# VectorE operands of a token search moved from SBUF to PSUM, in an attention and mixture-of-experts kernel

## The chip, the cores and the metric

The kernel runs on one core of a Trainium2 chip. Times are device microseconds of a whole execution of that core; the median of several runs counts. TensorE multiplies matrices, VectorE and ScalarE do elementwise work, GpSimd does elementwise work and issues the transfers with row lists, SyncE issues the other transfers.

## The reference

Three layers on 3072 tokens of 512 values, in float32: windowed attention, a dense layer, and a layer of 8 experts. The last one matters here:

```python
logits = x @ w_gate                      # 3072 x 8
order = np.argsort(-flat)                # all (token, expert) pairs, largest first
for idx in order:
    tok, e = (int(idx) // E, int(idx) % E)
    if assigned[tok] >= 0 or counts[e] >= cap:   # cap = 384
        continue
    assigned[tok] = e
    counts[e] += 1
...
for e in range(E):
    mask = assigned == e
    h = np.maximum(x[mask] @ w1[e], 0.0)         # 384 x 512 @ 512 x 1024
    out[mask] = h @ w2[e]                        # 384 x 1024 @ 1024 x 512
```

So each expert gets exactly 384 tokens, in the order of the logits.

## The kernel before, in words

Attention and the dense layer come first, in eight units of 384 tokens. The experts follow. The assignment does not sort: it finds which expert is full first, and with which tokens, and repeats this for the experts that are left. One such search (`search`, from L619) goes through eight levels of 16 thresholds on the 32-bit key of each token's best logit. `z[:, l]` holds digit l of 128 x 24 tokens. A level is:

- VectorE compares all tokens with 16 thresholds, in two halves, giving `mk` (L630 at the first level, L632 later);
- TensorE counts by expert, six products into `cnt` (L637);
- VectorE subtracts the digit found from `z[:, l]` (L640), carries it into the next digit (L642), and takes the own columns of `cnt` into `csum` (L644);
- TensorE sums these into `ct`, four products (L647);
- VectorE finds the digit `d` (`full` L652, `td` L654, L656).

After the eighth level `assign` (from L672) takes the expert `em`, its number `EI` (L683), its tokens `S`, and their running sums `sc` (L685). TensorE turns the sums of the partitions into offsets `off` (L690, L691). VectorE masks the expert's logits (L695), and `choose` (L997) makes every token's next best expert and its digits; ScalarE writes these into `z` (L1015). Then the slot list: positions `pos`, the tokens `mine`, the tokens done so far, two comparisons `ge` (L719), `row`, `cm`, `jc` (L730), and `oh` (L735), six operations of 128 x 512. From `oh` and `jc` TensorE makes the list `li` in 24 products (L739); VectorE reads it into `IDX` (L741, L743). With `IDX` GpSimd gathers the tokens' rows (L770) and, at the end, scatters the results (L834).

One search runs beside the products of the expert before. These are 96 products of 128 x 384 for the hidden layer (L811 to L813) and 72 of 128 x 512 for the output (L827 to L829). `beside` steps through the search: a step's TensorE instructions are tied behind a given product of the experts (`issue_after`), after as many nominal nanoseconds of products as `GAPS` names. Each engine runs its own instructions in a fixed order; a planner sets that order when the kernel is built. `limit` lets the search run up to two experts ahead.

An expert's weights come as 16 loads of 256 KB once `EI` is known and a buffer is free. ScalarE rounds each to the leading part (L762), GpSimd subtracts it for the trailing part (L763; for expert 0 half of them on VectorE). ScalarE and VectorE split the hidden layer likewise (`hh` L816, `hl` L817) and the gathered tokens (`mxh` L778, `mxl` L779). A finished expert's middle result is read out by VectorE (`res`, L833).

In PSUM, the bank `pS` ("search") holds `cnt`, `ct` and `off`; `li` has a bank of its own in the same pool; all other operands of the search are in SBUF.

Of the kernel before, what the change touches and what calls it, by code (L numbers as in the profile page):

```python
# [9 lines left out]
F32 = mybir.dt.float32  # L10
# [13 lines left out]
GRP = 4                       # columns of a group in the search  # L24
AHEAD = 3                     # quarters of w_in split before the first hidden unit
LEAD = 8                      # products by which the attention runs ahead of the dense layers
PACE0, PACE = 5000, 6000      # of the experts' weight loads, and from a load to its split
LAT0, LAT = 5000, 6000
TW, TR = (16000, 14000, 12000), 2000    # of the transposes of an expert's tokens
GAPS = (1600, 500, 1500, 6000)          # what the vector engine needs between the steps of the search  # L30
# [7 lines left out]
def attn_mlp_moe(ctx, tc, qT, kP, v, w_in, w_out, w_outT, w_gate, w1, w2, out):  # L38
# [31 lines left out]
    # lifetimes: `late` lasts to the end of the dense layers, `early` to the last hidden unit, `att` to the  # L70
    # last attention unit
# [13 lines left out]
    # masks over [previous block | sinks | own block], added to the negated scores  # L85
# [12 lines left out]
    # rows of head 0 / head 1 of a pair among the sink rows  # L98
# [18 lines left out]
    # a float64 weight is two words; its leading 24 bits become hi + lo  # L117
    WIN, WO = {}, {}

    def leading(pairs, n):  # L120
        """float32 of float64 word pairs: exponent rebased (the leading words, as float32, scaled by a power of
        two, so that what is too small becomes zero), mantissa cut to 23 bits"""
# [55 lines left out]
    # before the first hidden unit the banks of the dense layers serve the attention too  # L178
# [236 lines left out]
    def gate(u, c, ys):  # L415
        """logits of a unit, by quarters of its columns"""
# [11 lines left out]
    def logits(u):  # L428
        """from the products with the leading and the trailing part of the weights; then the choice"""
# [11 lines left out]
    # logits of the last unit straight from its hidden layer, by w_out @ w_gate, so that its assignment  # L441
    # runs beside its second product
# [51 lines left out]
    def pair_steps(u, p):  # L494
        """one head pair: a transpose follows the scores of the next block, so that the softmax has its time"""
# [21 lines left out]
    # the weights come between the loads of the first unit, and are split as they are needed  # L517
# [97 lines left out]
    ct, off = pS[:, 128:144], pS[:, 160:162]  # L615

    EI, IDX, NXT = {}, {}, {0: (BEST, CH, Z)}

    def search(n, best, ch, z, S):  # L619
        """the expert with the largest threshold, by digits; its tokens above the threshold and at it"""  # L620
        d = None
        for l in range(8):
            # tokens at or above every threshold
# [10 lines left out]
            # their number for every expert, by column of the group, then their sums  # L634
            for g in range(NJ // GRP):
                gs = slice(g * GRP, (g + 1) * GRP)
                nc.tensor.matmul(cnt, ch[:, gs].rearrange("p j e -> p (j e)"), mk[:, gs], start=(g == 0),  # L637
                                 stop=(g == NJ // GRP - 1))
            if l:
                dve.tensor_scalar(z[:, l], z[:, l], d, None, op0=OP.subtract)  # L640
            if l < 7:
                dve.scalar_tensor_tensor(z[:, l + 1], z[:, l], 16.0, z[:, l + 1], op0=OP.mult, op1=OP.add)  # L642
# [5 lines left out]
            # the digit of every expert's own search, then the largest  # L648
# [8 lines left out]
        # the expert  # L657
        es = wk.tile([P, E], F32, name="es")
        em = wk.tile([P, 1], F32, name="em")
        dve.scalar_tensor_tensor(es, td[:, :E], d, K["rank"], op0=OP.is_equal, op1=OP.mult)  # L660
        dve.tensor_reduce(em, es, AX.X, OP.max)
        # its tokens: above the threshold, at it
        above = wk.tile([P, NJ], F32, name="above")
        dve.tensor_scalar(above, z[:, 7], 16.0, d, op0=OP.mult, op1=OP.subtract)
# [7 lines left out]
    def assign(n, best, ch, z):  # L672
        """the next expert to fill up, and its tokens; what the next search needs"""
# [3 lines left out]
        else:  # L677
            # the rest is the last one's
# [5 lines left out]
        sc = wk.tile([P, 2, NJ], F32, name="sc")  # L684
        dve.tensor_tensor_scan(sc.rearrange("p h j -> p (h j)"), K["one1"], S.rearrange("p h j -> p (h j)"), 0.0,  # L685
# [6 lines left out]
        if n < E - 1:  # L692
            e1 = wk.tile([P, E], F32, name="e1")
            dve.tensor_scalar(e1, es, em, None, op0=OP.is_equal)
            dve.scalar_tensor_tensor(lm, e1[:, None, :].to_broadcast(V3), GONE, lm, op0=OP.mult, op1=OP.add)  # L695
            nxt = NXT[n + 1] = (wk.tile([P, NJ], F32, name="best"), wk.tile(V3, BF, name="ch"),
                   wk.tile([P, 8, NJ], F32, name="z", bufs=1))
            choose(nc, wk, K, lm, *nxt)
            z0 = nxt[2][:, 0]
            if n:  # L700
                dve.tensor_sub(z0, z0, done)
        # the first of those at the threshold, until it is full
        pos = wk.tile([P, 2, NJ], F32, name="pos")
        mine = wk.tile([P, NJ], F32, name="mine")
        dve.scalar_tensor_tensor(pos[:, 1], sc[:, 1], off[:, 1:2], S[:, 1], op0=OP.add, op1=OP.mult)
# [343 lines left out]
```

## Time and profile before

| | |
|---|---|
| median of 3 runs | 1345.03 us (1343.74 to 1352.11) |
| span of the profiled execution | 1342.2 us |
| TensorE busy in it | 1189.4 us (89%) |
| VectorE busy | 907.2 us (68%) |
| ScalarE busy | 606.9 us (45%) |
| GpSimd busy | 541.1 us (40%) |

The profile names lines as L632 and tiles as `mk<-z,d,steps`, which is output, then inputs. PE is TensorE, PEld its weight load, DVE VectorE, ACT ScalarE, POOL GpSimd. PEclk is the clock that was granted to TensorE, as a part of the full one. A time in brackets is what the engine waited before the instruction, and for whom. Windows are microseconds from the start of the span. "x7" is a run of seven instructions merged into one row.

### The profile page before, as it was taken

To read this page: it belongs to the slowest core of one execution; us is meant where nothing else is said; L and a number is where in the kernel's file an instruction comes from. 1 tells how busy PE (TensorE), PEld (TensorE's weight loads), DVE (VectorE), ACT (ScalarE), POOL (GpSimd) and SP (SyncE) were. 2 spreads that over 40 slices of the span, in tenths; PEclk is the share of its full clock that TensorE was granted. 3 is DMA by queue.
4 is the path that set the end of the run, shared out by engine and by line. 5 is a ranking of instruction groups with operands and counts; after the bars stand their busy time and mean duration, and the time that the engine had idled before them with its cause. 6 is when DMAs were issued, how large, how long until landed. Compare 5 with 4: busy or idle time off the path is not lost.

```text
span 1342.2 us, 19655 instructions
## 1 busy us (share of the span) xinstructions
PE 1189.4 (89%) x6484; PEld 979.2 (73%) x6484; DVE 907.2 (68%) x2320; ACT 606.9 (45%) x1436; POOL 541.1 (40%) x614
## 2 busy tenths in 40 slices
PE   4677899999999999999999999978759698787997
PEld 3466688888887878788888888646537476566996
DVE  7988976667667777756666545678777787776221
ACT  5755455566556556555566544033123241322411
POOL 6457633324334433523323310056262653725710
PEclk9988899999899999999999999979779798797999
DMA  6554433333424334333323220354142341434300
GB/s 223 169 178 150 165 126 93 97 90 124 114 95 128 118 102 124 112 86 93 98 89 95 76 71 1 103 172 148 49 126 73 101 142 63 142 104 132 110 24 24
DMA packets 87606, 145.29 MB, mean 108 GB/s; under 512 B 9680, under 2 KB 32208, under 8 KB 87504
## 3 DMA queue, kind: packets, MB, share of 16 engines
q1 hardware_dynamic: 83664, 131.45, 31.5%
q0 software_dynamic: 3840, 12.59, 2.8%
q8 instruction: 51, 0.84, 0.2%
q14 instruction: 51, 0.42, 0.1%
HBM read 127.22 MB, written 16.78 MB: 107 GB/s over the span
## 4 chain that ended last, share of the span: by engine, by line
PE 56%; DVE 23%; issue 8%; DMA 7%; POOL 3%; ACT 2%; SPq 1%; POOLq 0%; DVEq 0%; ACTq 0%
PE h L373 6%; PE h L371 5%; PE h L372 5%; PE y L400 5%; PE y L401 5%; PE y L399 5%; PE o L349 4%; DMA wtr<-in_w_outT_dram 3%; DVE mk L632 3%; PE h L811 2%; DMA wraw<-in_w_dram 2%; PE h L812 2%; PE t L317 2%; PE h L813 2%; DVE f L129 2%
## 5 line engine op out<-in xcount | busy, mean ns | idle before, releaser
L763 POOL TENSOR_TENSOR w<-wraw,w 128x512 fp32r<-128x512 f32 x120 | 171.0, 1458 | 185.7 <-ACT w L762 161.0
L371 PE MATMUL h<-xh,win 128*128 128x384 f32 x512 | 179.7, 352 | 0.7 <-ACT xh L361 0.7
L373 PE MATMUL h<-xh,win 128*128 128x384 f32 x512 | 178.7, 349 | 0.0
L372 PE MATMUL h<-xl,win 128*128 128x384 f32 x512 | 176.5, 345 | 0.0
L401 PE MATMUL y<-wo,gl 128*128 128x512 f32 x336 | 141.0, 421 | 1.6 <-DVE gl L385 1.6
L400 PE MATMUL y<-wl,gh 128*128 128x512 f32 x336 | 136.1, 405 | 0.0
L399 PE MATMUL y<-wo,gh 128*128 128x512 f32 x336 | 135.9, 405 | 0.0
L298 POOL TENSOR_SCALAR a<-a,stat 128x260 f32<-128x260 f32 (+2 forms) x168 | 87.2, 532 | 101.6 <-DVE stat L290 73.3
L286 ACT ACTIVATE a<-sm,stat 128x260 f32<-128x260 f32 (+2 forms) x192 | 94.6, 493 | 54.4 <-DVE stat L285 51.6
L816 ACT ACTIVATE hh<-h 128x384 fp32r<-128x384 f32 x64 | 31.4, 490 | 181.4 <-PE h L813 177.6
L262 POOL TENSOR_TENSOR vs<-vr,vs 128x192 fp32r<-128x192 f32 (+1 forms) x64 | 51.3, 809 | 145.7 <-ACT vs L261 145.3
L371 PEld LDWEIGHTS h<-xh,win 128*128 128x128 f32 x512 | 98.9, 193 | 6.4 <-ACT xh L361 1.6
L372 PEld LDWEIGHTS h<-xl,win 128*128 128x128 f32 x512 | 98.8, 193 | 5.4 <-issue 0.8
L378 DVE TENSOR_TENSOR g<-h,g 128x384 f32<-128x384 f32 x128 | 70.7, 552 | 44.5 <-ACT g L377 44.3
L373 PEld LDWEIGHTS h<-xh,win 128*128 128x128 f32 x512 | 98.5, 192 | 2.7 <-issue 1.8
L285 DVE CUSTOM_DVE_ANT_0 sm<-s,m 128x260 f32<-128x260 f32 (+2 forms) x192 | 76.5, 400 | 34.2 <-PE s L277 28.2
L811 PE MATMUL h<-mxh,w 128*128 128x384 f32 x256 | 97.9, 385 | 0.0
L762 ACT CAST w<-wraw 128x512 fp32r<-128x512 f32 x128 | 75.5, 619 | 46.5 <-DMA wraw<-in_w_dram 43.7
L248 POOL TENSOR_TENSOR kl<-k,kh 128x388 fp32r<-128x388 f32 (+1 forms) x64 | 84.5, 1327 | 26.7 <-ACT kh L247 26.3
L812 PE MATMUL h<-mxl,w 128*128 128x384 f32 x256 | 95.2, 373 | 0.0
L813 PE MATMUL h<-mxh,w 128*128 128x384 f32 x256 | 94.3, 369 | 0.0
L377 ACT ACTIVATE g<-h 128x384 f32<-128x384 f32 x128 | 62.1, 485 | 68.5 <-PE h L373 59.6
(257 smaller groups left out, 2996.7 us busy)
## 6 DMA issues: line engine op xcount, KB each, us to landing
wl<-wol_d SPq DMA_DIRECT2D x128, 256.0 KB, 2.9
wraw<-in_w_dram SPq DMA_DIRECT2D x128, 256.0 KB, 3.1
k<-in_k_dram SPq DMA_DIRECT2D x64, 131.0 KB, 2.9
winr<-in_w_in_dram SPq DMA_DIRECT2D x8, 1024.0 KB
wor<-in_w_out_dram SPq DMA_DIRECT2D x8, 1024.0 KB, 5.4
wtr<-in_w_outT_dram SPq DMA_DIRECT2D x8, 1024.0 KB
k<-in_k_dram SPq DMA_DIRECT2D x64, 97.0 KB, 2.5
q<-in_q_dram SPq DMA_DIRECT2D x32, 192.0 KB, 2.6
```

Source lines behind the costliest of these rows:

```text
L286: nc.scalar.activation(a[:, hh, :n], sm[:, :n], AF.Exp, bias=r[:, 0, hh:hh + 1], scale=-1.0, accum_out=r[:, 1, hh:hh + 1])
L298: nc.gpsimd.tensor_scalar(a[:, j, :n], a[:, j, :n], r[:, 3, j:j + 1], 1.0, op0=OP.mult, op1=OP.mult)
L371: nc.tensor.matmul(hp, w, xh[:, c], start=(c == 0), stop=False)
L372: nc.tensor.matmul(hp, w, xl[:, c], start=False, stop=False)
L373: nc.tensor.matmul(hp, win(f, 1, c), xh[:, c], start=False, stop=(c == NC - 1))
L399: yield 213, nc.tensor.matmul(y, gh[:, ts], hi, start=(f == 0), stop=False)
L400: yield 213, nc.tensor.matmul(y, gh[:, ts], lo, start=False, stop=False)
L401: yield 213, nc.tensor.matmul(y, gl[:, ts], hi, start=False, stop=(f == NF - 1))
L763: (dve if n == 0 and q % 2 else nc.gpsimd).tensor_sub(t[:, 1], r, raw(t)[:, 0])
L811: nc.tensor.matmul(hp, w1h[:, c], xh[:, c], start=(c == 0), stop=False)
L812: nc.tensor.matmul(hp, w1h[:, c], xl[:, c], start=False, stop=False)
L813: yield 480, nc.tensor.matmul(hp, w1l[:, c], xh[:, c], start=False, stop=(c == NC - 1))
```

## The change

Operands of the search move from SBUF to PSUM, so that operations with two tensors have one in each memory. A new bank `hold` (`pH`) takes `z`, `dg`, `val`, `best`, `row`, `above` and a copy of `rank`; the free columns of the bank `search` (`pS`) take the slot list `li`, copies of `shift` and of the scan's ones, `e1`, `sc`, `pos`, `mine`, `cm` and `em`. The bank that `li` had is given up. `z[:, l]` less the digit goes to a new SBUF tile `zd` instead of back into `z`. Two sums of SBUF pairs become reductions over a pair (`either`, `g2`). The tokens done are subtracted from the next `z` once, after they have been added up, so the subtraction of L701 goes. `row` becomes float32. Comments go as well. The core of the diff:

```diff
-    ct, off = pS[:, 128:144], pS[:, 160:162]
-
-    EI, IDX, NXT = {}, {}, {0: (BEST, CH, Z)}
+    ct, off, li = pS[:, 128:144], pS[:, 160:162], pS[:, 176:176 + 2 * NT].rearrange("p (h t) -> p h t", h=2)
...
+    pH = psS.tile([P, 512], F32, name="hold")
...
+    zH, dgH = held(pH, 0, 8, NJ), held(pH, 192, 8, NJ).bitcast(I32)
+    valH, bestH = held(pH, 384, NJ), (held(pH, 408, NJ), held(pH, 432, NJ))
+    rowH, aboveH, rankH = held(pH, 456, NJ), held(pH, 480, NJ), held(pH, 504, E)
+    oneS, e1S, shiftS = held(pS, 64, 2 * NJ), held(pS, 112, E), held(pS, 120, 8).bitcast(I32)
+    scS, pos1S, posS = held(pS, 192, 2, NJ), held(pS, 240, NJ), held(pS, 264, NJ)
+    mineS, cmS, emS = held(pS, 288, NJ), held(pS, 312, NJ, NT), held(pS, 384, 1)
+    for d, x in ((rankH, K["rank"]), (shiftS, K["shift"]), (oneS, K["one1"]), (zH, Z)):
+        nc.vector.tensor_copy(d, x)
+    KP = dict(K, rank=rankH, shift=shiftS)
+
+    EI, IDX, NXT = {}, {}, {0: (BEST, CH, zH)}
...
+            zd = wk.tile([P, NJ], F32, name="zd")
             if l:
-                dve.tensor_scalar(z[:, l], z[:, l], d, None, op0=OP.subtract)
+                dve.tensor_scalar(zd, z[:, l], d, None, op0=OP.subtract)
+            else:
+                dve.tensor_copy(zd, z[:, l])
             if l < 7:
-                dve.scalar_tensor_tensor(z[:, l + 1], z[:, l], 16.0, z[:, l + 1], op0=OP.mult, op1=OP.add)
+                dve.scalar_tensor_tensor(z[:, l + 1], zd, 16.0, z[:, l + 1], op0=OP.mult, op1=OP.add)
...
-        em = wk.tile([P, 1], F32, name="em")
-        dve.scalar_tensor_tensor(es, td[:, :E], d, K["rank"], op0=OP.is_equal, op1=OP.mult)
+        em = emS
+        dve.scalar_tensor_tensor(es, td[:, :E], d, rankH, op0=OP.is_equal, op1=OP.mult)
...
-        above = wk.tile([P, NJ], F32, name="above")
-        dve.tensor_scalar(above, z[:, 7], 16.0, d, op0=OP.mult, op1=OP.subtract)
+        above = aboveH
+        dve.tensor_scalar(above, zd, 16.0, d, op0=OP.mult, op1=OP.subtract)
...
-        sc = wk.tile([P, 2, NJ], F32, name="sc")
-        dve.tensor_tensor_scan(sc.rearrange("p h j -> p (h j)"), K["one1"], S.rearrange("p h j -> p (h j)"), 0.0,
+        sc = scS
+        dve.tensor_tensor_scan(sc.rearrange("p h j -> p (h j)"), oneS, S.rearrange("p h j -> p (h j)"), 0.0,
                                op0=OP.mult, op1=OP.add)
...
-            e1 = wk.tile([P, E], F32, name="e1")
+            e1 = e1S
...
-            nxt = NXT[n + 1] = (wk.tile([P, NJ], F32, name="best"), wk.tile(V3, BF, name="ch"),
-                   wk.tile([P, 8, NJ], F32, name="z", bufs=1))
-            choose(nc, wk, K, lm, *nxt)
-            z0 = nxt[2][:, 0]
-            if n:
-                dve.tensor_sub(z0, z0, done)
...
+            nxt = NXT[n + 1] = (bestH[n % 2], wk.tile(V3, BF, name="ch"), zH)
+            choose(nc, wk, KP, lm, *nxt, val=valH, dg=dgH)
+            z0 = zH[:, 0]
+
+        either = wk.tile([P, NJ], F32, name="either")
+        mine, pos = mineS, posS
+        dve.scalar_tensor_tensor(pos1S, sc[:, 1], off[:, 1:2], S[:, 1], op0=OP.add, op1=OP.mult)
+        dve.tensor_reduce(either, S.rearrange("p h j -> p j h"), AX.X, OP.add)
+        dve.scalar_tensor_tensor(mine, pos1S, CAP + 0.5, either, op0=OP.is_lt, op1=OP.mult)
         if n < E - 1:
-            dve.tensor_sub(z0, z0, mine)
             dve.tensor_add(done, done, mine)
+            dve.tensor_sub(z0, z0, done)
...
+        pos0 = wk.tile([P, NJ], F32, name="pos0")
+        dve.scalar_tensor_tensor(pos0, sc[:, 0], of0, S[:, 0], op0=OP.add, op1=OP.mult)
+        dve.tensor_add(pos, pos0, pos1S)
...
-        dve.tensor_add(g2, ge[:, 0], ge[:, 1])
-        row = wk.tile([P, NJ], BF, name="row")
-        dve.scalar_tensor_tensor(row, g2, -float(P), pos[:, 0], op0=OP.mult, op1=OP.add)
-        cm = wk.tile([P, NJ, NT], F32, name="cm", bufs=1)
+        dve.tensor_reduce(g2, ge.rearrange("p h j -> p j h"), AX.X, OP.add)
+        row = rowH
+        dve.scalar_tensor_tensor(row, g2, -float(P), pos, op0=OP.mult, op1=OP.add)
+        cm = cmS
         dve.tensor_sub(cm[:, :, 0], mine, ge[:, 0])
-        dve.tensor_sub(cm[:, :, 1], ge[:, 0], ge[:, 1])
+        dve.scalar_tensor_tensor(cm[:, :, 1], pos, 2 * P + 0.5, ge[:, 0], op0=OP.is_lt, op1=OP.mult)
...
-        li = psS.tile([P, 2, NT], F32, name="li")
...
-def choose(nc, pool, K, lm, best, ch, z):
+def choose(nc, pool, K, lm, best, ch, z, val=None, dg=None):
...
-    dg = pool.tile(D3, I32, name="dg", bufs=1)
-    nc.vector.tensor_tensor(dg, u[:, 1:2].to_broadcast(D3), K["shift"][:, :, None].to_broadcast(D3),
+    sh = pool.tile(D3, I32, name="dg", bufs=1)
+    if dg is None:
+        dg = sh
+    nc.vector.tensor_tensor(sh, u[:, 1:2].to_broadcast(D3), K["shift"][:, :, None].to_broadcast(D3),
                             op=OP.logical_shift_right)
     nc.vector.tensor_reduce(best, eq, AX.X, OP.max)
-    nc.vector.tensor_scalar(dg, dg, 15, None, op0=OP.bitwise_and)
+    nc.vector.tensor_scalar(dg, sh, 15, None, op0=OP.bitwise_and)
```

## Rows read from the trace of the kernel before

**Rows 1.** Busy us by engine (and instructions) per window, PEclk, DMA share, GB/s.

```profile
800.00:868.00 68.00, 68.00 (x403) 53.44 (x402) 37.92 (x139) 18.21 (x40) 0.12 (x1) 1.00 0.16 46
868.00:900.00 32.00, 22.69 (x139) 15.24 (x138) 27.64 (x89) 11.74 (x21) 19.23 (x11) 0.81 0.64 212
900.00:1250.00 350.00, 283.00 (x1613) 213.93 (x1612) 260.70 (x761) 97.29 (x187) 172.25 (x133) 0.85 0.33 105
1250.00:1342.00 92.00, 84.36 (x429) 75.68 (x427) 15.68 (x28) 21.29 (x42) 27.16 (x25) 0.98 0.16 52
```

**Rows 2.** Waits of TensorE, 900 to 1250 us: total us, times, longest.

```profile
PE search L637 <- DVE mk L632: 24.7, 6, 8.2
PE li L739 <- DVE oh L735: 19.2, 10, 6.5
PE search L647 <- DVE csum L644: 14.4, 5, 4.9
```

**Rows 3.** VectorE groups, 800 to 868 us: busy us, mean ns, idle before.

```profile
L632 DVE SCALAR_TENSOR_TENSOR mk<-Z,d,steps 128x192 bf16<-128x192 f32 x14 | 5.2, 416 | 0.3
...
L644 DVE TENSOR_TENSOR csum<-search,own 32x64 f16<-32x64 f32 x8 | 1.7, 212 | 0.8 <-PE search L637 0.8
...
L640 DVE TENSOR_SCALAR Z<-Z,d 128x24 f32<-128x24 f32 x7 | 1.7, 238 | 0.2
```

**Rows 4.** VectorE groups, 900 to 1250 us.

```profile
L632 DVE SCALAR_TENSOR_TENSOR mk<-z,d,steps 128x192 bf16<-128x192 f32 x74 | 60.6, 860 | 1.2
L735 DVE TENSOR_TENSOR oh<-slots,row 128x512 bf16<-128x512 bf16 x42 | 37.5, 956 | 0.0
L640 DVE TENSOR_SCALAR z<-z,d 128x24 f32<-128x24 f32 x38 | 25.2, 663 | 0.8
L817 DVE SCALAR_TENSOR_TENSOR hl<-h,hh 128x384 fp32r<-128x384 f32 x45 | 24.6, 547 | 15.5 <-ACT hh L816 15.2
...
L644 DVE TENSOR_TENSOR csum<-search,own 32x64 f16<-32x64 f32 x43 | 9.0, 210 | 20.7 <-PE search L637 20.2
...
L701 DVE TENSOR_TENSOR z<-z,done 128x24 f32<-128x24 f32 x6 | 6.5, 1086 | 2.0 <-ACT z L1015 2.0
...
L1005 DVE TENSOR_TENSOR eq<-LG,val 128x192 f32<-128x192 f32 x6 | 2.1, 350 | 0.0
```

**Rows 5.** Timelines of VectorE, GpSimd, TensorE around one stop: start, us.

```profile
937.67 9.15 DVE L632 SCALAR_TENSOR_TENSOR mk<-z,d,steps 128x192 bf16<-128x192 f32 x2
...
937.70 8.58 POOL L763 TENSOR_TENSOR w<-wraw,w 128x512 fp32r<-128x512 f32 x7
...
946.55 0.32 PE L637 MATMUL search<-mk,ch 128*32 128x64 bf16 x3 [8.23 <-DVE mk L632]
```

**Rows 6.** Windows after that stop, and a later one.

```profile
948.00:957.00 9.00, 9.00 (x38) 6.33 (x37) 3.98 (x18) 0.97 (x2) 0.00 (x0) 0.56 0.01 2
957.00:967.00 10.00, 10.00 (x68) 6.49 (x66) 6.95 (x29) 2.13 (x5) 1.09 (x2) 1.00 0.00 0
...
1034.00:1044.00 10.00, 9.20 (x70) 6.30 (x70) 7.90 (x19) 6.17 (x12) 10.00 (x5) 1.00 0.50 173
```

**Rows 7.** Timelines of TensorE and VectorE in one slot list.

```profile
1034.50 0.26 PE L739 MATMUL li<-jc,oh 128*128 128x6 bf16 x4 [0.54 <-DVE oh L735]
...
1035.36 0.26 PE L637 MATMUL search<-mk,ch 128*32 128x64 bf16 x3
...
1033.77 3.69 DVE L735 TENSOR_TENSOR oh<-slots,row 128x512 bf16<-128x512 bf16 x6
...
1039.39 0.16 DVE L743 SCALAR_TENSOR_TENSOR idx<-li,ls 128x3 int32<-128x3 f32 x1
```

**Rows 8.** VectorE's timeline: ends of two experts, a search's result.

```profile
1102.82 0.68 DVE L833 COPY res<-o 128x512 f32<-128x512 f32 x1
...
1135.34 0.13 DVE L683 TENSOR_SCALAR ei<-em 1x1 int32<-1x1 f32 x1
...
1165.42 0.68 DVE L833 COPY res<-o 128x512 f32<-128x512 f32 x1
```

More of the change, by code (lines that the diff above doesn't have):

```diff
@@ L614, in attn_mlp_moe, with held @@
     cnt = pS[:GRP * E, :GRP * 16].rearrange("p (j k) -> p j k", k=16)
-    ct, off = pS[:, 128:144], pS[:, 160:162]
-    EI, IDX, NXT = {}, {}, {0: (BEST, CH, Z)}
+    ct, off, li = pS[:, 128:144], pS[:, 160:162], pS[:, 176:176 + 2 * NT].rearrange("p (h t) -> p h t", h=2)
+    pH = psS.tile([P, 512], F32, name="hold")
+    def held(tile, at, *shape):
+        t = tile[:, at:at + int(np.prod(shape))]
+        return t.rearrange("p (a b) -> p a b", b=shape[1]) if len(shape) == 2 else t
+    zH, dgH = held(pH, 0, 8, NJ), held(pH, 192, 8, NJ).bitcast(I32)
[8 more added lines that the diff above has]
+    EI, IDX, NXT = {}, {}, {0: (BEST, CH, zH)}
     def search(n, best, ch, z, S):
@@ L700, in assign @@
-            if n:
-                dve.tensor_sub(z0, z0, done)
-        pos = wk.tile([P, 2, NJ], F32, name="pos")
-        mine = wk.tile([P, NJ], F32, name="mine")
-        dve.scalar_tensor_tensor(pos[:, 1], sc[:, 1], off[:, 1:2], S[:, 1], op0=OP.add, op1=OP.mult)
-        dve.tensor_add(mine, S[:, 0], S[:, 1])
-        dve.scalar_tensor_tensor(mine, pos[:, 1], CAP + 0.5, mine, op0=OP.is_lt, op1=OP.mult)
+            nxt = NXT[n + 1] = (bestH[n % 2], wk.tile(V3, BF, name="ch"), zH)
+            choose(nc, wk, KP, lm, *nxt, val=valH, dg=dgH)
@@ L711, in assign @@
         of0 = wk.tile([P, 1], F32, name="of0")
         dve.tensor_copy(of0, off[:, 0:1])
[L715 to L716 removed]
+        pos0 = wk.tile([P, NJ], F32, name="pos0")
+        dve.scalar_tensor_tensor(pos0, sc[:, 0], of0, S[:, 0], op0=OP.add, op1=OP.mult)
+        dve.tensor_add(pos, pos0, pos1S)
         ge = wk.tile([P, 2, NJ], F32, name="ge")
         for h in range(2):
[L719 removed]
+            dve.tensor_scalar(ge[:, h], pos, P * (h + 1) + 0.5, None, op0=OP.is_ge)
@@ L994, in search_consts @@
     return K
-def choose(nc, pool, K, lm, best, ch, z):
+def choose(nc, pool, K, lm, best, ch, z, val=None, dg=None):
     n, E = lm.shape[1], lm.shape[2]
     V3, D3 = [P, n, E], [P, 8, n]
-    val = pool.tile([P, n], F32, name="val", bufs=1)
+    if val is None:
+        val = pool.tile([P, n], F32, name="val", bufs=1)
     nc.vector.tensor_reduce(val, lm, AX.X, OP.max)
```

3 lines of the change are left out of this document (removed).

## The prediction, made before the change was run

> **What bounds the kernel now.** I read the busy time by stretches first [rows 1], because the share of TensorE over the whole span (89%) hides one stage. Up to 868 us TensorE never stops and its clock is granted in full. From 900 to 1250 us, where the experts' products run with the next search between them, TensorE is busy 283.0 of 350 us: it stands still for 67.0 us, and its mean granted clock is 0.85. From 1250 us, with no search left, it is busy 84.36 of 92 us at 0.98. So the experts' stage loses time twice: by stops, and by the lower clock.
>
> Who ends the stops is in the waits [rows 2]: the three largest, 58.3 us together, end on VectorE: on `mk` (the comparison with the 16 thresholds), on `oh` (the slot list's one-hot) and on `csum`. TensorE runs in order, so a search product whose operand is late holds up the experts' products behind it.
>
> Why VectorE is late shows when its groups of 800 to 868 us, where GpSimd is busy 0.12 us [rows 1], are set beside those of 900 to 1250 us, where GpSimd splits weights for 172.25 us [rows 3, 4]. `mk` goes from 416 to 860 ns, the subtraction from `z` (L640) from 238 to 663 ns. `csum` does not change (212 and 210 ns), and `hl` stays at 547 ns over 45 instructions. The ones that do not change read one operand from PSUM, the ones that grow read SBUF alone. One stop in full [rows 5]: two `mk` take 9.15 us from 937.67, seven GpSimd splits run back to back for 8.58 us from 937.70, and TensorE waits 8.23 us. VectorE got in when GpSimd had nothing queued. [...]
>
> The excess: `mk` 74 x (860 - 416) ns = 32.9 us; L640 38 x (663 - 238) = 16.2; `oh` 42 x (956 - 615) = 14.3, with 3.69 us / 6 = 615 ns from a run without a pause [rows 7]; L701 6 x (1086 - about 180) = 5.4. That is 68.8 us, about TensorE's 67.0. These are two readings of one loss, not two losses.
>
> The clock [rows 6]: behind the stop of rows 5 it is 0.56 from 948 to 957 us, 38 products in 9 us, though TensorE is busy throughout; from 957 to 967 us it is 1.00 and 68 products run in 10 us. [...] Over the stage this costs 283.0 x (1 - 0.85) = 42.5 us.
>
> **The change, part by part.** (1) `z`, `rank`, `shift`, the ones of the scan, `best`, `val`, `dg`, `sc`, `pos`, `mine`, `row` and `cm` move to PSUM, so that each VectorE operation of searches 1 to 6 that had two SBUF operands, and the single-operand ones that grew (L640 `z`, L719 `ge`), now has one in PSUM or becomes a reduction (`either`, `g2`). By rows 4 such operations are not delayed, `csum` and `hl` being the witnesses. If so, all of the 67.0 us of stops falls to what is late without GpSimd.
>
> (2) What a PSUM operand costs when read. `csum` (64 columns, 210 ns) and `hl` (384 columns, 547 ns) both read PSUM and give 1.05 ns a column; at 192 columns that line is at 345 ns, and a two-SBUF operation of 192 columns, L1005, takes 350 [rows 4]. I take nothing. [...]
>
> (3) What a PSUM result costs: VectorE writes to PSUM nowhere in this trace. Some 22 operations a search now do. From below nothing; from above I allow a second fixed part, 210 - 64 x 1.05 = 143 ns, so 22 x 143 = 3.1 us a search, 22 us over seven. I take nothing, the lower end: the nearest rows show no difference between the memories in reading, and most of these results lie where TensorE has other products in front of it.
>
> (4) Moves and additions. L701 (6, with 5.4 us of excess already counted) goes; seven copies of a 24-column `z` and four copies at the start come, all of the size of `csum` or less except the first `z` (192 columns, under 0.4 us): 2 us of VectorE spread over the stage and hidden by products. `dg` loses its faster form, at most 0.1 us a search.
>
> (5) The shared bank. `e1` is now written to the bank into which the offsets' product goes, so `e1`, the masking of the logits and `val` start after that product instead of beside it: three operations of at most 350 ns [rows 4], 1.05 us a search. Behind them stand the choice, the slot list and `oh`, for which TensorE already waits 0.54 us in the undisturbed search [rows 7]; the 0.9 us that L701 loses there pays for most. `ch` now stands behind ScalarE's write of `z`. I take 1 us of stop for each of seven searches: 7 us.
>
> (6) GpSimd gains too: its splits took 8.58 / 7 = 1.23 us when VectorE was the one waiting [rows 5]. Before 900 us TensorE is idle 32.0 - 22.69 = 9.3 us [rows 1], mostly for the first weights and tokens; earlier splits may give 2 us.
>
> (7) The clock. A stop of 0.54 us left it at 1.00 from 1034 to 1044 us [rows 6, 7], so stops of about 1 us should not cost what those of 8 us do. I take back 30 of the 42.5 us.
>
> The sum against this execution's span, 1342.2 us: - 67.0 + 7 - 30 - 2 = - 92, a span of 1250. The median of the runs, 1345.03 us, is 2.8 us above the span, so **1253 us**.
>
> What is next: at full clock the stage's products fill 283.0 x 0.85 = 241 of today's 350 us, so an expert that takes 1165.42 - 1102.82 = 62.6 us today [rows 8] would take 43 us. VectorE without its excess has (260.70 - 68.8) x 62.6 / 350 = 34 us of work for an expert, GpSimd 16 x 1.23 = 20 us of splits besides its transfers. TensorE stays the bound. Of the search itself: counted from 0, expert 5 is known at 1135.34, when TensorE has 30 us of expert 3 left [rows 8], so the weights have time.
>
> **The rivals.** *PSUM is dear after all* (reads, writes or both): 22 us by the bound of (3), and the stops that this leaves keep the clock down, so that 15 of the 30 us do not come back either: 1253 + 22 + 15 = 1290 us. [...] For it: no row shows a VectorE write to PSUM. Against it: rows 4.
>
> *The stall stays*: what holds VectorE is not its second SBUF operand but its SBUF result, or GpSimd's activity as such. `mk` still writes SBUF. Then only the additions remain: 1345 + 2 + 7 = 1354 at the worst, 1345 at the best. Against it: `csum` and `hl` write SBUF too and are not held.
>
> *The other side: the shared bank makes the search the bound.* Today the counts of the next search run among the products of the slot list: the first at 1035.36, while the list is read only at 1039.39 [rows 7]. With both in one bank the counts must wait until the list has been read, 4 us, and likewise each VectorE operation in the bank waits for TensorE's, each in queue order behind other products. It decides where the new waits eat the whole gain: 92 / 7 = 13 us a search, three times the 4 us of the hand-over. At 16 us a search it is 1253 + 7 x 16 = 1365 us. [...] For it: TensorE is in order, so a wait for the bank stops the experts too. Against it: inside the eight levels nothing new touches that bank; only the hand-over between searches does, once each.
>
> **How the numbers follow.** Forecast (1225 to 1275): 0.72. PSUM dear (1275 to 1330): 0.14. Stall stays: 0.05. Search bound by the bank: 0.09. The low end takes all of the clock, all of the start and no new stop: 1342.2 - 67 - 42.5 - 9.3 + 2.8 = 1226; I set 1230. The high end is the dear rival's 1290. Between them lie the 0.72 and most of the 0.14. About 1% is what a measurement of this kernel can tell from no change: faster by more 0.86, within it 0.05, slower 0.09.
>
> **What would show it.** Right: `mk` and the subtraction from `z` near 0.42 and 0.24 us while GpSimd splits; TensorE's waits on `mk`, `oh` and `csum` under 15 us together; the granted clock of the experts' stage above 0.93; GpSimd's split near 1.23 us; an expert every 43 to 46 us. Wrong in size: operations with a PSUM result over 0.3 us at 24 columns; the first slot product waiting 2 us or more for `oh`. Wrong in kind: `mk` still at several us beside a run of splits, or TensorE waiting on search products for VectorE operations that wait for the bank.

## The result, and the profile after

The changed kernel takes 1307.04 us (median of 4 runs, 1302.52 to 1308.70), the kernel before 1344.38 us beside it: a ratio of 0.9745, with a 95% interval of 0.9703 to 0.9787. It is faster, by 37 us instead of the 92 that were forecast, and lies above the range of 1230 to 1290 us. The profiled execution has a span of 1300.5 us, against 1342.2 before.

The first view of the kernel after is the busy time by stretches, with the columns of [rows 1].

```profile
868.00:900.00 32.00, 19.29 (x122) 13.31 (x121) 23.43 (x81) 12.41 (x23) 14.40 (x11) 0.79 0.60 205
900.00:1210.00 310.00, 272.02 (x1642) 206.04 (x1641) 182.40 (x765) 96.53 (x181) 150.49 (x128) 0.92 0.36 114
1210.00:1300.50 90.50, 79.14 (x405) 67.87 (x403) 15.95 (x30) 23.06 (x45) 33.91 (x30) 0.95 0.22 68
```

In the experts' stage TensorE still stands still for 310.00 - 272.02 = 38.0 us (67.0 before), at a clock of 0.92 (0.85 before). From 868 us to the end, idle time goes from 84 to 62 us. The clock's loss, busy time x (1 - PEclk) summed over the windows, goes from 48.5 to 29.8 us. That is 22 + 19 = 41 us and answers for the 42 us by which the span is shorter. Some 4 us of this had come about ahead of the experts, where both kernels have the same products: the hundredth product from the end of the dense layer starts at 851.8 us before and at 847.4 us after.

VectorE's groups from 900 to 1250 us, as in [rows 4], show that the stall is gone:

```profile
L835 DVE SCALAR_TENSOR_TENSOR hl<-h,hh 128x384 fp32r<-128x384 f32 x54 | 29.7, 552 | 18.2 <-ACT hh L834 17.7
L650 DVE SCALAR_TENSOR_TENSOR mk<-hold,d,steps 128x192 bf16<-128x192 f32 x78 | 28.9, 413 | 1.4
L753 DVE TENSOR_TENSOR oh<-slots,hold 128x512 bf16<-128x512 bf16 x42 | 27.4, 678 | 0.0
...
L665 DVE TENSOR_TENSOR csum<-search,own 32x64 f16<-32x64 f32 x44 | 9.3, 211 | 26.1 <-PE search L655 26.0
L659 DVE TENSOR_SCALAR zd<-hold,d 128x24 f32<-128x24 f32 x39 | 9.1, 234 | 0.0
...
L663 DVE SCALAR_TENSOR_TENSOR hold<-zd,hold 128x24 f32<-128x24 f32 x38 | 7.0, 183 | 0.6
```

`mk` is at 413 ns beside GpSimd's splits (860 before), and the subtraction of the digit at 234 ns (663 before).

TensorE's waits of 900 to 1250 us, as in [rows 2], show what has taken the stall's place:

```profile
PE xt L793 <- DMA yg<-y_d,idx: 37.5, 10, 6.6
PE search L757 <- DVE jc L749: 2.1, 3, 1.0
PE o L845 <- ACT hh L834: 1.1, 1, 1.1
```

The waits on `mk`, `oh` and `csum`, 58.3 us before, are not there any more. Instead TensorE waits 37.5 us, ten times, to transpose (`xt`) the tokens that GpSimd's indirect transfer gathers (`yg`). One of these stops, from the timelines of VectorE, GpSimd and TensorE after:

```profile
983.33 0.16 DVE L761 SCALAR_TENSOR_TENSOR idx<-search,ls 128x3 int32<-128x3 f32 x1
...
973.47 16.39 POOL L781 TENSOR_TENSOR w<-wraw,w 128x512 fp32r<-128x512 f32 x13 [18.75 <-ACT w L780]
990.02 0.99 POOL L788 DMA_INDIRECT yg<-y_d,idx  x1 [0.15 <-issue]
...
988.06 0.26 PE L655 MATMUL search<-mk,ch 128*32 128x64 bf16 x3
993.52 0.45 PE L793 MATMUL xt<-ident,yg 128*128 128x128 f32 x1 [5.21 <-DMA yg<-y_d,idx]
```

The list of rows (`idx`) is ready at 983.5 us. GpSimd is in a run of 13 weight splits until 989.86 us, and the gather stands behind them in its queue: it starts 0.16 us after the thirteenth. So the transfer starts 6.5 us late, and TensorE stands still for 5.21 us.

Behind this stop the granted clock is 0.68 for 9.5 us and then 1.00, in two windows of the kernel after (columns of [rows 1]):

```profile
993.50:1003.00 9.50, 9.42 (x47) 6.79 (x47) 4.66 (x20) 1.93 (x4) 3.76 (x4) 0.68 0.15 47
1003.00:1013.00 10.00, 10.00 (x65) 7.21 (x64) 6.72 (x28) 2.54 (x5) 2.95 (x3) 1.00 0.21 78
```

The late gather is not new. From GpSimd's timeline of the kernel before, beside the list of [rows 7] that was ready at 1039.55 us, and all of TensorE's waits for gathered tokens in that execution:

```profile
1045.29 3.70 POOL L763 TENSOR_TENSOR w<-wraw,w 128x512 fp32r<-128x512 f32 x3
1049.15 0.97 POOL L770 DMA_INDIRECT yg<-y_d,idx  x1 [0.17 <-DVE csum L644]
...
PE xt L775 <- DMA yg<-y_d,idx: 0.9, 2, 0.6
```

There it was 9.6 us late (of experts 1 to 6, two others 8.3 and 6.4 us and the rest about 1 us) and cost next to nothing. By the start times in the trace, 43 to 91 of the experts' products lay between a list's last product and the first transpose of its tokens, for experts 1 to 6. After the change 13 to 20 do. And 12 or 13 of the expert's 16 splits stand ahead of its gather, where it was 8 to 10. Why the planner's order came out so was not looked into.

### The profile page after: what moved, and what is told of

Same layout as the page of the kernel before. It is cut to its first block, busy times and chain, and to the rows that moved or that the text cites. A ratio compares the mean times of both kernels' runs of the same rounds, so it can differ in the third digit from the quotient of the medians.

```text
span 1300.5 us, 19669 instructions
## 1 busy us (share of the span) xinstructions
PE 1169.5 (90%) x6484; PEld 959.2 (74%) x6484; DVE 827.2 (64%) x2325; ACT 608.3 (47%) x1436; POOL 521.2 (40%) x614
## 4 chain that ended last, share of the span: by engine, by line
PE 58%; DVE 15%; DMA 11%; issue 6%; POOL 5%; ACT 2%; SPq 1%; POOLq 0%; DVEq 0%; ACTq 0%
PE h L373 6%; PE h L371 5%; PE y L401 5%; PE h L372 5%; PE y L399 5%; PE y L400 5%; DMA wraw<-in_w_dram 4%; PE o L349 4%; POOL w L781 3%; DMA wtr<-in_w_outT_dram 3%; DVE f L129 2%; PE t L317 2%; PE h L830 2%; DMA yg<-y_d,idx 2%; PE h L831 2%
## 5 line engine op out<-in xcount | busy, mean ns | idle before, releaser
L781 POOL TENSOR_TENSOR w<-wraw,w 128x512 fp32r<-128x512 f32 x120 | 151.9, 1302 | 152.1 <-ACT w L780 120.4
L276 PE MATMUL s<-kh,qs 128*128 128x260 f32 (+2 forms) x192 | 61.8, 324 | 34.2 <-DVE stat L285 26.3
L831 PE MATMUL h<-mxh,w 128*128 128x384 f32 x256 | 91.7, 358 | 0.0
```

The lines of the kernel that those rows point to most:

```text
L781: (dve if n == 0 and q % 2 else nc.gpsimd).tensor_sub(t[:, 1], r, raw(t)[:, 0])
L831: yield 480, nc.tensor.matmul(hp, w1l[:, c], xh[:, c], start=False, stop=(c == NC - 1))
```

## The experiments

Three theories stood at first. A: the gather's place in GpSimd's queue takes the gain. B: the slot list, longer by the hand-over in the shared bank, takes it. C: TensorE's products stand in an order that gives the list no cover. Two questions were added later: what the change costs in itself, and what held VectorE.

### The gather ahead of half of the splits

```diff
-            split_w(*parts.pop(0)[1:])
+            _, n, q, a = parts[0]
+            if n and q * NC + a >= 8:
+                if n not in GA:
+                    break
+                with tc.issue_after(GA[n].ins):
+                    split_w(*parts.pop(0)[1:])
+            else:
+                split_w(*parts.pop(0)[1:])
```

`GA[n]` is the gather of expert `n`. The loads may also run six ahead from the first expert on.

> The changed kernel, with one thing moved: in GpSimd's queue the token gather of the next expert stands behind 8 of the 16 weight splits of that expert instead of 12 or 13. Theory A (queue): the missing gain lies in the gather, which the changed kernel issues 6.5 us after the slot list is read because it stands behind splits; then the gather is issued within 2 us of the list, TensorE's waits on gathered rows fall from 44 us to under 12, part of the low clock comes back, and the time is 1307 - 33 - 12 = about 1262 us. Theory B (list): the shared banks make the slot list longer, and that is what TensorE waits for; then the gather comes no earlier than the list allows, at most a third of the waits goes and the time stays above 1290. Theory C (products): TensorE is bound by its products and the order of the search, and the gather only shows where it happens to stop; the stop turns up elsewhere and the time stays within 1% of 1307.

Measured: 1271.94 us (1270.29 to 1273.01), ratio to the kernel before 0.9472 (0.9434 to 0.9510). The window, the wait that is left (900 to 1210 us), and the timelines where the stop was:

```profile
900.00:1210.00 310.00, 294.64 (x1810) 224.68 (x1809) 191.05 (x788) 111.98 (x214) 177.90 (x151) 0.98 0.41 129
...
PE xt L793 <- DMA yg<-y_d,idx: 7.3, 9, 1.8
...
983.72 0.16 DVE L761 SCALAR_TENSOR_TENSOR idx<-search,ls 128x3 int32<-128x3 f32 x1
...
973.91 10.11 POOL L781 TENSOR_TENSOR w<-wraw,w 128x512 fp32r<-128x512 f32 x8 [18.63 <-ACT w L780]
984.66 0.98 POOL L788 DMA_INDIRECT yg<-y_d,idx  x1 [0.65 <-PE h L831]
...
988.56 0.30 PE L793 MATMUL xt<-ident,yg 128*128 128x128 f32 x1 [0.54 <-DMA yg<-y_d,idx]
```

The list is ready when it was; the gather follows it by 0.8 us; the stop of 5.21 us is one of 0.54 us. TensorE's stops in the stage fall from 38.0 to 15.4 us and its clock rises from 0.92 to 0.98. From the running sums to `idx` the lists of experts 1 to 6 take 13.1 to 15.1 us, against 13.1 to 14.7 in the changed kernel, so nothing of the 35 us goes to theory B; 13 to 18 products still lie between a list and its transposes, so nothing goes to C. In neither kernel does TensorE wait for weights in the stage, so the loads that may run ahead are not the cause either. The 35 us are theory A's, though its number, 1262 us, was 10 us too low.

### The slot list shortened

```diff
-    rowH, aboveH, rankH = held(pH, 456, NJ), held(pH, 480, NJ), held(pH, 504, E)
-    oneS, e1S, shiftS = held(pS, 64, 2 * NJ), held(pS, 112, E), held(pS, 120, 8).bitcast(I32)
+    rowH, aboveH, rankH = held(pH, 456, NJ), valH, held(pH, 504, E)
+    oneS, e1S, shiftS = held(pS, 64, 2 * NJ), held(pH, 480, E), held(pH, 488, 8).bitcast(I32)
...
+    nc.vector.tensor_tensor(ch, eq, best[:, :, None].to_broadcast(V3), op=OP.is_equal)
     nc.scalar.activation(z, dg, AF.Copy, scale=0.0625)
-    nc.vector.tensor_tensor(ch, eq, best[:, :, None].to_broadcast(V3), op=OP.is_equal)
```

So `e1` and `shift` leave the bank into which the offsets' product goes, and `ch` no longer stands behind ScalarE's write of `z`.

> The changed kernel with the hand-over made shorter: e1 and shift lie in the bank that TensorE does not write, so the choice does not wait for the offsets' product, and ch is formed ahead of ScalarE's write of z. The queue of GpSimd is not touched on purpose. Theory A (queue): the splits in front of the gather end when they did (they start with the expert's number), so the gather is issued at the same distance behind the expert's number and the time stays within 1% of 1307 us, though the list is read 2 to 3 us earlier. Theory B (list): the list from the sums (r) to idx falls from 14.5 to about 12 us, the stops by 2 to 3 us each, seven of them, so 1307 - 17 - 5 = about 1285 us.

Measured: 1303.77 us (1299.72 to 1307.71), ratio 0.9706 (0.9660 to 0.9753): not to be told from the change itself. TensorE's wait, and VectorE's timeline from the running sums to the list:

```profile
PE xt L793 <- DMA yg<-y_d,idx: 31.5, 7, 6.4
...
977.19 0.16 DVE L709 CAST r<-search 128x2 bf16<-128x2 f32 x1
978.11 0.23 DVE L715 TENSOR_SCALAR hold<-es,search 128x8 f32<-128x8 f32 x1 [0.77 <-PE search L712]
...
990.24 0.16 DVE L761 SCALAR_TENSOR_TENSOR idx<-search,ls 128x3 int32<-128x3 f32 x1
```

This takes 13.1 us; it was 968.84 to 983.33 = 14.5 us in the changed kernel and 11.8 us in the kernel before. A list that comes 1.4 us earlier still waits for the same splits. But over experts 1 to 6 the list became only 0.4 us shorter (13.9 to 13.5 us in the mean), as VectorE's waits from 868 to 1300 us explain, first in the changed kernel, then here:

```profile
DVE ch L1037 <- ACT hold L1036: 11.5, 7, 2.7
...
DVE hold L728 <- ACT hold L1037: 9.7, 5, 3.1
```

The wait for ScalarE's write of `z` moved from `ch` to the subtraction of the tokens done (L728), which stands ahead of the list too. And `e1` (L715) still waits for the offsets' product, because `em`, which it reads, stayed in that bank. So this run does not test theory B; the early gather rules it out, since there the 35 us come with lists as long as before.

### Both edits, and the gather still earlier

> Both edits together: shorter hand-over and the gather behind 8 splits. Theory A: the queue was the bound and the list is next, so 5 to 15 us below the run with the early gather alone, about 1250 us, what the prediction summed to. Theory B: the sum of two small gains, about 1270. If products are the bound (C): 1307.

Measured: 1267.75 us (1263.93 to 1271.61), ratio 0.9448 (0.9407 to 0.9488). It is the fastest version that leaves nothing out, 39 us below the changed kernel. The 4 us that the list's edits add to the early gather lie within both intervals. That is theory B's number for this run (about 1270 us), not A's (about 1250). As the list is hardly shorter, whether it is the next bound stays open.

In the next version the gather goes behind 4 splits instead of 8:

```diff
-            if n and q * NC + a >= 8:
+            if n and q * NC + a >= 4:
```

> The version with the mended slot list and the gather ahead of the later splits, with the gather now behind 4 splits instead of 8. Theory A (the gather's place in GpSimd's queue): up to 4 x 1.3 = 5 us earlier for each gather if its list is ready by then; but TensorE's waits for xt were down to 9.5 us in 11 pieces of at most 1.9 us, so that much of the rest is the transfer itself (3.5 us from issue to landing) and not the queue. Expected 1260 to 1268 us; if the list is ready later than the fourth split, GpSimd stands idle for it and the splits behind come late: above 1275 us with waits for w.

Measured: 1273.42 us (1269.50 to 1276.20), ratio 0.9482 (0.9442 to 0.9522). The waits for `xt` (850 us to the end) are 8.3 us, against 9.5. The time lies between the two that were named, and its interval overlaps that of the version with 8 splits. So a place still earlier in the queue gives nothing that can be told; what is left of the waits, 1.9 us at most, is by the author's estimate by and large the transfer, which takes 3.5 us from issue to landing in the changed kernel.

### The early gather in the kernel before

> The kernel before with the edit of gather_early alone: the token gather is issued behind 8 of the 16 splits of its expert's weights. Theory A (the gather's place in GpSimd's queue became the limit only in the changed kernel, where 12 to 13 splits stand ahead of it and TensorE reaches the transposes 13 to 18 products behind the list; before, 8 to 10 splits and 44 to 91 products): within 1% of before, 1328 to 1350 us, since TensorE's waits for xt are small there already. If early gathering were a gain of its own, whatever the operands: 1310 us or less, as from 1307 to 1272 us in the changed kernel.

Measured: 1341.10 us (1337.06 to 1350.33), ratio 1.0009 (0.9972 to 1.0047). The edit that gives 35 us in the changed kernel gives nothing in the kernel before. It is a weak test, as there it moves a gather ahead of two splits at most, and the gathers of experts 1 to 6 are still up to 8.4 us late, where it was 9.6. The stronger sign is the kernel before itself: late gathers, and 0.9 us of waiting for them. The late gather became a cost only when the order of the changed kernel took its cover away.

### The levels alone

The edit to the kernel before; the slot list shares the counts' bank too, and its other operands stay in SBUF:

```diff
-    EI, IDX, NXT = {}, {}, {0: (BEST, CH, Z)}
+    pH = psS.tile([P, 512], F32, name="hold")
+    zH = pH[:, :8 * NJ].rearrange("p (a b) -> p a b", b=NJ)
+    nc.vector.tensor_copy(zH, Z)
+    EI, IDX, NXT = {}, {}, {0: (BEST, CH, zH)}
...
-                dve.tensor_scalar(z[:, l], z[:, l], d, None, op0=OP.subtract)
+                dve.tensor_scalar(zd, z[:, l], d, None, op0=OP.subtract)
...
-                dve.scalar_tensor_tensor(z[:, l + 1], z[:, l], 16.0, z[:, l + 1], op0=OP.mult, op1=OP.add)
+                dve.scalar_tensor_tensor(z[:, l + 1], zd, 16.0, z[:, l + 1], op0=OP.mult, op1=OP.add)
```

> The kernel before with only the eight levels changed: z in a PSUM bank (with zd in SBUF), the list's products in the counts' bank so that there is room, everything else of the search in SBUF as before. mk and the subtraction should fall to 0.42 and 0.24 us in all searches, while oh stays near 0.95 us. The excess removed is 49 of 69 us. If stops fall in proportion and the slot list keeps its old length: about 1345 - 0.7 x 60 = 1300 us. If the whole gain of the change came from the levels: 1307 or below. If the list's operations carry it: above 1325.

Measured: 1316.30 us (1310.37 to 1328.47), ratio 0.9785 (0.9740 to 0.9830). TensorE's waits from 900 to 1210 us:

```profile
PE search L744 <- DVE oh L740: 23.6, 13, 6.0
PE xt L780 <- DMA yg<-y_d,idx: 7.2, 2, 6.8
PE search L744 <- DVE jc L736: 7.0, 1, 7.0
```

The time lies between the numbers that were named. The stall has moved on to the operations that still have two operands in SBUF, `oh` above all, on which 23.6 us of these waits end, 6.0 us at the longest. So the list's operands have to move too, and the step to the whole change gives only 1316 to 1307 us, with the gather as the new wait. The levels alone already bring part of the new order: 15 to 65 products lie between list and transposes (experts 1 to 6).

### What held VectorE

GpSimd's split is replaced by an operation that only writes SBUF (the splits that VectorE had for expert 0 as well):

```diff
-        (dve if n == 0 and q % 2 else nc.gpsimd).tensor_sub(t[:, 1], r, raw(t)[:, 0])
+        nc.gpsimd.memset(raw(t)[:, 1], 0.0)
```

> The kernel before, with each GpSimd split (a subtraction of two SBUF operands, result to SBUF) replaced by a memset of the same trailing half, which only writes SBUF; VectorE's operations and their operands are those of before. The experts' trailing halves are zero, so they are left out of the sum; the products and transfers stay. Theory R (VectorE and GpSimd hold SBUF's reading side in turn when VectorE reads two operands there): with no GpSimd reads the stall goes: mk near 0.42 us and the subtraction from z (L640) near 0.24 us in 900 to 1250 us, TensorE's waits on mk, oh and csum together under 10 us instead of 58. Theory G (GpSimd's activity as such, or its writes, hold VectorE): mk stays well above 0.6 us wherever memsets run, and long stops remain; the excess shrinks only with GpSimd's busy time. Time: theory R about 1250 to 1275 us if the stops and most of the clock come back, theory G above 1300 us unless the memset is far shorter than 1.23 us.

Measured: 1257.01 us, one run, in an order that the planner set anew for the shorter operation. VectorE's groups from 900 to 1250 us, then one place in its timeline and GpSimd's:

```profile
L632 DVE SCALAR_TENSOR_TENSOR mk<-z,d,steps 128x192 bf16<-128x192 f32 x72 | 27.0, 417 | 1.2
...
L640 DVE TENSOR_SCALAR z<-z,d 128x24 f32<-128x24 f32 x37 | 22.2, 600 | 0.8
...
896.47 8.04 DVE L640 TENSOR_SCALAR z<-z,d 128x24 f32<-128x24 f32 x1
...
895.87 1.06 POOL L770 DMA_INDIRECT yg<-y_d,idx  x1 [0.30 <-issue]
896.93 7.54 POOL L763 MEMSET w<- 128x512 f32 x16
```

`mk` lies beside a memset ten times from 868 us on and takes at most 0.42 us each time; beside a split of the kernel before it took up to 8.83 us. Two others with two tensors in SBUF are short too in the mean: `oh` at 685 ns (956 in the kernel before), the carry of the digit (L642) at 180 (249). So for these three theory R holds: with no GpSimd reads their stall is gone. For the subtraction from `z` (L640), which has one tensor in SBUF and its result there too, theory R's number fails: it stays at 600 ns, and TensorE still waits 10.8 us for `csum`, which stands behind it (under 10 us were named). From 868 us on, the 34 subtractions that meet no memset take at most 0.24 us, and of the eight that do, one takes 8.04 us and ends only when sixteen memsets in a row are over. That is a second kind of conflict, with operations that only write. What of L640 meets the memsets no row shows.

What the long waits have in common is the issue of an indirect transfer. L640 began at 896.47 us, while GpSimd issued a gather, and the memsets followed without a pause; the two next longest (2.78 and 2.52 us) began in such an issue too, and beside memsets alone L640 took at most 0.61 us. In the kernel before, nine VectorE operations from 868 us on took over 2 us. Six began in such an issue and three in the run of splits directly behind one; the stop of [rows 5] is one of the six:

```profile
936.74 0.95 POOL L770 DMA_INDIRECT yg<-y_d,idx  x1 [0.30 <-issue]
```

In other runs of splits VectorE got in after at most two, within 1.77 us. Why VectorE is kept out of the runs behind an issue was not tried; in the run with memsets no `mk` met the end of an issue.

With the move to PSUM neither is held beside a split: in the changed kernel 22 `mk` of the later levels (L650) take at most 0.419 us, and 11 subtractions (L659) at most 0.235 us. The changed kernel was not run with memsets.

### The price of the change in itself

The split is left out, so that GpSimd neither holds VectorE nor delays the gather:

```diff
-        (dve if n == 0 and q % 2 else nc.gpsimd).tensor_sub(t[:, 1], r, raw(t)[:, 0])
...
-        w1h, w1l = w[:, 0, :, fs], w[:, 1, :, fs]
+        w1h, w1l = w[:, 0, :, fs], w[:, 0, :, fs]
...
-        w2h, w2l = w[:, 0, f % 4], w[:, 1, f % 4]
+        w2h, w2l = w[:, 0, f % 4], w[:, 0, f % 4]
```

First in the kernel before:

> The kernel before without any split of the experts' weights (products use the leading part twice, the trailing part is left out; the number of products and all transfers stay). This prices the prediction's sum itself: what the kernel before gains if GpSimd never stands in VectorE's way and the token gather never stands behind a split. The sum of the prediction says stops of 67 us and most of 42.5 us of clock come back: 1345 - 92 - 7 (no shared bank here) = about 1245 us. If the kernel before has other waits behind the stall, that the prediction did not see, it stays above 1280 us. mk should be near 0.42 us in 900 to 1250 us by both theories on the stall, and waits for xt (the gathered tokens) near 0.

Measured: 1240.50 us (1238.95 to 1242.87), ratio 0.9251 (0.9187 to 0.9315). The window:

```profile
900.00:1210.00 310.00, 304.56 (x1897) 245.31 (x1896) 182.06 (x751) 113.65 (x220) 41.71 (x42) 0.99 0.39 131
```

So the stall and the clock behind it were worth what the sum said, with the caution that the planner sets the order anew where there is no split. Then in the changed kernel:

> The changed kernel without any split of the experts' weights (products use the leading part twice, the trailing part is left out; the number of products and all transfers stay). Against the kernel before without splits (1240.5 us) this prices what the change itself adds where GpSimd neither holds VectorE nor keeps the token gather waiting: PSUM operands, shared bank, added operations, and the planner's new order. Theory A (the changed kernel lost only by the gather behind the splits): 1240 to 1255 us, the upper end if the shared bank costs the 1 us a search of the prediction and the list its 2.7 us, since in this order the transposes follow 13 to 18 products behind the list; waits for xt under 12 us together. Theory P (the change's own parts are dear, in PSUM or in the bank): 1270 us or more, with waits for search operands instead of xt.

Measured: 1264.67 us (1261.76 to 1267.39), ratio 0.9430 (0.9392 to 0.9468). That is 24 us more, between the two theories' numbers. TensorE's waits from 900 to 1210 us are small:

```profile
PE xt L792 <- DMA yg<-y_d,idx: 5.4, 7, 3.2
PE xt L792 <- issue: 1.0, 3, 0.4
PE search L757 <- DVE jc L749: 1.0, 2, 0.8
```

Two steps between them, both without splits. The first has only the shared bank, the second the levels too:

> The kernel before with the slot list in the counts' bank (before_li), and without any split of the experts' weights (the trailing part is left out, as in before_nosplit and after_nosplit, 1240.5 and 1264.7 us). Without GpSimd's splits a wait for the bank can't hide behind the stalls. The changed kernel is 24 us dearer than the kernel before in this form; the question is which part of the change carries it. Theory B (the shared bank): 1255 to 1265 us. Theory O (the slot list's other edits and the planner's order that goes with them, one whole expert of 168 products for a search instead of some 140): 1238 to 1248 us.

> levels_only (z and zd in PSUM for the eight levels, slot list in the counts' bank, everything else of the list in SBUF) without any split of the experts' weights. Theory L (the levels' PSUM operands cost time in themselves): above li_nosplit by 8 us or more. Theory O (the slot list's edits and the order, not the levels): within 5 us of li_nosplit, about 1240 to 1250 us, since mk at 413 ns and the subtraction at 234 ns are as short as their SBUF forms (417 and 242 ns without splits).

Measured: 1243.26 us (1238.64 to 1247.51), ratio 0.9249 (0.9204 to 0.9293), and 1256.04 us (1253.54 to 1257.00), ratio 0.9348 (0.9316 to 0.9380). By these medians the bank carries some 3 us (the runs overlap with those without it), the levels some 13, the rest of the list some 9. For the levels theory L's number came (above the bank alone by 8 us or more), yet not by the durations of operations: VectorE's groups from 868 to 1200 us with the levels in PSUM are

```profile
L635 DVE SCALAR_TENSOR_TENSOR mk<-hold,d,steps 128x192 bf16<-128x192 f32 x84 | 31.2, 413 | 1.4
...
L644 DVE TENSOR_SCALAR zd<-hold,d 128x24 f32<-128x24 f32 x42 | 9.8, 234 | 0.0
...
L658 DVE TENSOR_SCALAR_CACHE_REDUCE full<-search 128x15 f32<-128x15 f32 (+1 forms) x48 | 8.3, 173 | 36.7 <-PE search L653 31.4 <-PE h L817 3.2 <-issue 2.1
```

and with them in SBUF 416, 238 and 173 ns. What changes with each step is the order as built: from one search's offsets to the next there are 134 to 168 of the experts' products in the kernel before without splits, 137 to 168 with the bank, 143 to 148 with the levels, 168 in the changed kernel without splits. The spans of the profiled executions of the two ends differ by 23.5 us, but 6 us of that had come about ahead of the experts: the hundredth product from the end of the dense layer starts at 847.9 and 854.2 us, and over all fourteen profiled executions between 846.9 and 854.2 us, whichever operands the search has. From there to the end it is 390.0 us in the kernel before, 395.3 with the bank, 405.0 with the levels and 407.2 in the changed kernel, all without splits. So a profile gives 17 us where the medians give 24, and 5, 10 and 2 us for the three steps; the size of each step is uncertain by several us. Of the 17 us, 5 are TensorE's idle time and 12 its busy time, for the same number of products and at a mean granted clock of 0.97 in both. Whether the order is the cause was not tried.

The bank with the splits in place:

```diff
-    ct, off = pS[:, 128:144], pS[:, 160:162]
+    ct, off, li = pS[:, 128:144], pS[:, 160:162], pS[:, 176:176 + 2 * NT].rearrange("p (h t) -> p h t", h=2)
...
-        li = psS.tile([P, 2, NT], F32, name="li")
```

> The kernel before with the slot list li put into the counts' bank, and nothing else. The prediction priced the shared bank at 1 us of stop per search (7 us); its rival at 13 us or more a search (90 us). Theory B small: within 1% of before, 1335 to 1352 us. Theory B large (rival): 1400 us or more. The first product of li should wait for nothing new, and the first counts of the next search stand behind the read of li.

Measured: 1345.66 us (1339.85 to 1359.72), ratio 1.0042 (0.9998 to 1.0085). The rival of 13 us a search is out as far as the hand-over of `li` goes; a wait of 1 us a search lies inside the interval. `e1` and the other operands that the change puts into that bank are not in this run; in the changed kernel itself TensorE's waits for VectorE on search products come to 2.1 us from 900 to 1250 us.

## Why the prediction was wrong

**Right: the stall and where it goes (part 1).** `mk` at 413 and the subtraction at 234 ns are the numbers that were named, and the waits on `mk`, `oh` and `csum` fell from 58.3 us to nothing that shows. The kernel before without splits, at 1240.5 us, confirms the sum's large terms, 67 us of stops and 30 of clock, taken together (about 1245 by the same working). The rival that the stall stays falls. Two readings on the way were off without harm. "Up to 868 us TensorE never stops" holds only for 800 to 868 us; from 0 to 800 us it was busy 731 us. And the excess of `oh` set the mean of single operations, 956 ns, against a run's time shared out, 615 ns; undisturbed, single ones take 687 ns in the mean in the kernel before without splits, so that the excess is 11.3 and not 14.3 us, and the sum 65.8 and not 68.8.

**Right: reading and writing PSUM (parts 2 and 3).** The subtraction from PSUM takes 234 ns, that from SBUF 238 [rows 3]. `mk` takes 413 against 416. L663, with its result in PSUM, takes 183 ns, and its SBUF form 179 in the kernel before without splits. `dg` (L1035, 192 columns), with its result in PSUM, takes 350 ns where it took 250 (L1014), the 0.1 us a search that part 4 named. So the rival "PSUM is dear" has next to no durations behind it, although 1307 us lies in the stretch that was given to it (1275 to 1330): the number is near, the cause is another.

**About right: the shared bank (part 5).** The hand-over of `li` costs some 3 us without splits and 0 to 11 us with them, no number that can be told from nothing. The waits that the part itself named are there, `e1` for the offsets' product and `ch` behind ScalarE's write of `z`; what they cost TensorE no run shows by itself.

**Wrong: "What is next".** This step set GpSimd down as "20 us of splits besides its transfers", a busy time for an expert, and concluded that TensorE stays the bound and that the weights have time. It asked of the weights whether they come in time and not of the tokens. The tokens' gather stands in the same queue as the splits, and the trace of before had it up to 9.6 us behind its list. The step took it for granted that the order around the search stays as it was; instead the search stretches over a whole expert, and the transposes come 13 to 20 products behind the list. The missing term is TensorE's wait for `xt`, 37.5 us in the stage, with the clock that such stops keep down: the prediction had no term for it. Putting the gather ahead of half of the splits gave 35 us back.

**Mis-sized: the clock (part 7).** 19 us came back instead of 30, because the new stops are up to 6.6 us long: in the 9.5 us behind the one of 5.21 us the clock is at 0.68. With the early gather, where no stop in the stage is over 2.1 us, it is at 0.98, above the 0.93 that was forecast. The step was right for short stops; the stops were not short.

**Mis-sized: the additions (parts 4 and 5 together).** Without splits the change costs 24 us by the medians (17 by the profiled executions, counted from the dense layer's end) where 7 to 9 were set. The list grew by 2.7 us instead of 1.05 in the case compared above (by 3.1 us in the mean of experts 1 to 6 without splits); in that list `ch` waits 2.50 us for ScalarE and `e1` 0.77 us for the offsets' product. The edits that were to end these waits mostly moved them and gave 3 to 4 us, less than the runs can tell, so the price of the longer list is not measured. TensorE's waits without splits are small, and most of the price is the busy time told above. Its cause stays open.

**Wrong, and small: the start (part 6).** TensorE's idle time from 868 to 900 us went from 9.3 to 12.7 us instead of falling by 2.

Together, of the 54 us between 1253 and 1307, 39 are the gather and the list's edits (1307.04 to 1267.75). The other 15 are of the size by which the additions exceed their price, and open like it.

## What to carry to other kernels

Before you credit a removed stall, list what else is queued on the engines that the stall kept slow, find for each transfer they issue when its input is ready and how much work lies between it and its consumer, and ask whether the change keeps that cover. An instruction that is late at no cost in the trace of before (here a gather 9.6 us behind its list) can be the next bound once its consumer moves up. When GpSimd works on SBUF in long runs, consider one operand of VectorE's short operations in PSUM (here `mk` went from 860 to 413 ns), and put GpSimd's transfers ahead of its long work (here 35 us). Price the move by itself, in a version without the conflict: here it cost 17 to 24 us of what it gained.

## What was not expected of the hardware

VectorE was held beside GpSimd not for one instruction but for a whole run of them: 9.15 us for two `mk` beside seven splits [rows 5], and 8.04 us for one `tensor_scalar` of 24 columns beside sixteen memsets. In these two executions, for each VectorE operation of over 2 us from 868 us on, GpSimd was issuing or had just issued an indirect transfer, with the run directly behind it. A memset on GpSimd's side left `mk`, with two operands in SBUF, alone (ten of ten at 0.42 us or less), but not the `tensor_scalar` from SBUF to SBUF (8.04 us). VectorE wrote 24 float32 columns to PSUM in 183 ns, about as fast as to SBUF (179 ns).
